# Scores and values of an attention on array tiles of 64 rows by 32 columns in place of 64 by 64

## The chip, the core and the metric

The kernel runs on one core of a Trainium2 chip. The metric is device time in microseconds (us) of one launch; the kernel before took 578.21 us, the median of 3 runs (577.76 to 578.54). TensorE (PE in the profile, its weight loads PEld) multiplies matrices and writes to the accumulators in PSUM, VectorE is DVE, ScalarE ACT, GpSimd POOL, and SyncE (SP) starts the DMAs.

## The reference, cut to what matters

Attention with a causal window of 128 positions and a linear bias, then a gated MLP over each batch. Batch 8, 8 heads, 576 positions, head dimension 64, all float32:

```python
scores = scale * np.matmul(q, k.transpose(0, 1, 3, 2))
rel = pos[:, None] - pos[None, :]
mask = (rel >= 0) & (rel < 128)
scores = np.where(mask, scores + bias[None], -1000000000.0)
attn = np.exp(scores - max); attn = attn / (sum + 1e-09)
x = (attn @ v), heads side by side                    # (8, 576, 512)
h = gelu(x @ w_in); u, v = halves of h
v_s = einsum('ts,bsd->btd', w_sg, layernorm(v) * g_ln) + b_sg
out = x + (u * v_s) @ w_out
```

## The kernel before, in words

The attention is done in 32 pairs of heads, numbered n: pair n is two heads of batch n // 4, one head on partitions 0 to 63 of the tile `qk` and the other on 64 to 127 (`heads`, L245). Queries are taken in nine blocks of R = 64. A query of a block can see the keys of its own block and of the two blocks before it, at most 192 keys. P is 128, T is 4.

`score_list` (L264) makes the products of a pair. Each is a `nc.tensor.matmul` of 64 rows (the head dimension) by 64 columns (the queries, as weights) by up to 192 streamed columns (the keys). So a product takes a quarter of the 128 by 128 array: the row half is the head's (`js`), the column half is given by where the result goes (`to`), and four products that differ in these use the four quarters. The list for `t2 = 0` has ten products: two of 128 columns, six of 192, two of 64 (the first block, which sees only itself); the list for `t2 = 2` has eight of 192. The results stand in two PSUM banks per list, the key window of the first block of queries (`i = 0`) in columns 0 to 191 and that of the second in 192 to 383.

`minima` (L297) has DVE merge the oldest and the newest 64 keys into one block of 64 (one of them is masked for each query), add the bias and take the minimum; then ACT takes exponentials, POOL or ACT scales them, PE transposes them (L347, L360), and DVE writes them, masked, to `px` (L356). `values` (L376) multiplies them by v: 18 products `part` and two products `first` per pair, each of 64 rows (64 keys), 64 columns (the head's 64 columns of v, as weights) and 64 to 192 streamed columns (queries), again on quarters: the row half by the key block's parity, the column half by the head j.

Weights and streamed data of scores and values are float32, and the trace has two weight loads and two matmuls (two passes) for each such product.

The other products are those of the MLP (L607 to L609, L796, L798, L905, L940, L941, L1059), on the whole array, 288 or 512 streamed columns.

The order of the work is a written list of steps, `ORDER` (L1150), in which a step is a letter and a pair: `*18` is both score lists of pair 18, `V16` the values of pair 16, `A`, `B`, `C`, `G` the four `minima`. Every engine takes its instructions in that order. For pairs 13 and 15 to 29 (`BEHIND`) the values of pair n come after the scores of pair n + 2 and one of their results is put in a free corner of that pair's score bank; for 15 to 29 no other product of PE stands between the two.

Of the kernel before, what the change touches and what calls it, by code (L numbers as in the profile page):

```python
# [21 lines left out]
def attention_gmlp(  # L22
# [17 lines left out]
    nc = tc.nc  # L40
    B, H, D, _, S = qkT.shape
    P = 128
# [4 lines left out]
    T = S // P  # L47
    R = S - T * P
    S2 = S // 2
    NPAIR = H // 2  # L50
    W = P
    EPS = 1e-6
# [20 lines left out]


    XW = 2 * S + R

    def hi_of(x):
        return x[:, 0:S]

    def lo_of(x):  # L80
        return x[:, S + R:XW]

# [10 lines left out]
    def halves(name, n, dt=F32):  # L93
        return const.tile([P, n], dt, name=name)
# [12 lines left out]
    alone, merged, plain = [rel[low, i * R:(i + 1) * R] for i in (0, 1, 2)]  # L107
# [9 lines left out]
    sel = halves("sel", 4 * R, U8)  # L117
# [4 lines left out]
    sel_first, sel = [sel[:, i * 2 * R:(i + 1) * 2 * R].rearrange("p (t c) -> p t c", t=2) for i in range(2)]  # L122

    biases = []
    for hp in range(NPAIR):
        x = halves(f"bias{hp}", 7 * R)
        nc.vector.tensor_scalar(x, rel, -slopes[2 * hp] * math.sqrt(D), None, ALU.mult)
        x = x.rearrange("p (b c) -> p b c", c=R)
# [17 lines left out]
    for i in range(2):  # L146
        x = const.tile([P, 2 * R], F32, name=f"e0_{i}")
# [5 lines left out]
    for i in range(3):  # L153
        x = const.tile([P, 2, NS], F32, name=f"stats{i}")
# [71 lines left out]
    def burst(insts):  # L226

        last = None
        for one in insts:
            if last is None:  # L230
                last = one()
            else:
                with tc.issue_after(last.ins):
                    last = one()

    class Pair:
# [26 lines left out]

        def score_list(self, t2, pool):  # L264
            qk, heads = self.qk, self.heads
            W = 3 * R
            if t2 == 0:
                self.pr = [att.tile([P, T, P], F32, name="e", bufs=4) for _ in range(2)]
                self.e0 = e0s[self.n % 2]
            if (self.n, t2) in IN_M:  # L270
                m = ps_m.tile([P, 2, 512], F32, name="ps_m")
                banks = self.banks[t2] = [m[:, i, :] for i in range(2)]
            else:
                banks = self.banks[t2] = [pool.tile([P, 512], F32, name=pool.name) for _ in range(2)]

            def score(half, j, c, q0, k0, k1):
                js, to = heads[j], heads[half ^ j]
                return lambda: nc.tensor.matmul(banks[half][to, c:c + k1 - k0], qk[js, 0, q0:q0 + R], qk[js, 1, k0:k1], start=True, stop=True)  # L278

            insts = []  # L280
            for i in range(2):
                for half in range(2):
                    for j in range(2):
                        q0 = (2 * t2 + 1 + i + 2 * half) * R
                        if q0 < P:
                            insts.append(score(half, j, i * W + R, q0, 0, P))
                        else:
                            insts.append(score(half, j, i * W, q0, q0 - P, q0 + R))
            if t2 == 0:
                insts += [score(0, j, 2 * W, 0, 0, R) for j in range(2)]  # L290
            return insts

        def shift(self, dst, src, bs, acc):
# [3 lines left out]
        def minima(self, t2, j):  # L297
            bank, pr, nm = self.banks[t2][j], self.pr, self.nm
            bias = biases[self.hp][j]
            sv = bank.rearrange("p (b c) -> p b c", c=R)  # L300
            alone = t2 + j == 0
            nc.vector.copy_predicated(sv[:, 0:6:5, :], sel_first if alone else sel, sv[:, 2:4, :])
            for i in range(2):
                bs = bias[:, 2:4, :] if i else bias[:, 0:3:2, :] if alone else bias[:, 1:3, :]
                self.shift(pr[j][:, t2 + i, :].rearrange("p (b c) -> p b c", b=2), sv[:, 4 * i:4 * i + 2, :], bs, nm[:, j * T + t2 + i:j * T + t2 + i + 1])
            if alone:
                self.shift(self.e0[:, R:P], sv[:, 6, :], bias[:, 0, :], nm[:, 2 * T:2 * T + 1])

        def exp(self, x, i):
            n = x.shape[0]  # L310
# [57 lines left out]
        def values(self):  # L368
            vt, px, heads = self.vt, self.px, self.heads
            if self.n in V_IN_S:  # L370
                x1 = [ps_s.tile([P, 512], F32, name="ps_s") for _ in range(2)]
            else:
                m = ps_m.tile([P, 2, 512], F32, name="ps_m")
                x1 = [m[:, i, :] for i in range(2)]
            self.x1 = x1
            behind = self.n in BEHIND  # L376
            x0 = self.x0 = pairs[BEHIND[self.n]].banks[2][1][:, 6 * R:7 * R] if behind else self.ct0[:, P:P + R]

            def part(k, j):
                i = 1 - k % 2  # L380
                rows, slot = slice(i * R, (i + 1) * R), (k + 1) // 2
                lo, hi = max(k - 1, 0), min(k + 2, 2 * T)
                c0 = (2 * P * (slot - 1) + P + i * R) if k else 0
                return lambda: nc.tensor.matmul(x1[i][heads[j], lo * R:hi * R], vt[rows, slot, heads[j]], px[rows, j * 2 * T * P + c0:j * 2 * T * P + c0 + (hi - lo) * R], start=k < 2, stop=k > 2 * T - 2, skip_group_check=True)  # L384

            def first(j):
                js, ks = heads[j], heads[1 - j if behind else 1]
                return lambda: nc.tensor.matmul(x0[js], vt[ks, 0, js], self.p0[ks, j * R:(j + 1) * R], start=True, stop=True)

            burst([part(k, j) for k in range(2 * T) for j in (1, 0)] + [x for j in (1, 0) for x in (part(2 * T, j), first(j))])  # L390

        def gather(self):
            nc.scalar.copy(self.xf[:, R:S], self.x1[0])
# [4 lines left out]
        def high(self):  # L398
            xs = self.xs = mlp.tile([P, XW], F32R, name="xs", bufs=NC)
            xss[self.b][self.hp] = xs  # L400
            nc.scalar.copy(hi_of(xs), self.xf)  # L401
# [4 lines left out]
        def low_tail(self):  # L406
# [7 lines left out]
            "R": inverse, "r": scale_first, "s": lambda p: p.scale(0), "S": lambda p: p.scale(1),  # L414
            "t": lambda p: p.transpose(0), "X": lambda p: p.masked(0), "z": transpose_first, "P": copy_first,
            "T": lambda p: p.transpose(1), "Y": lambda p: p.masked(1), "p": gather_first, "V": values, "x": gather, "2": gather_even, "h": high, "l": low, "k": low_tail,
        }

# [11 lines left out]
    class Planner:  # L430
# [7 lines left out]
        def add(self, name, engine, length, at, run, after=(), port=False, take=(), table=None, lag=0.22):  # L438
            assert name not in self.steps, name
            self.steps[name] = (engine, length, at, run, [x for x in after if x], port or engine == "POOL", list(take), table, lag)  # L440
# [688 lines left out]
    def idle_products(n, pool):  # L1129

        def run():
            if pool == "ps_m":
                m = ps_m.tile([P, 2, 512], F32, name="ps_m")
                banks = [m[:, i, :] for i in range(2)]
            else:
                banks = [{"ps_s": ps_s, "ps_a": ps_a}[pool].tile([P, 512], F32, name=pool)]
            for i in range(n):
                at = i // len(banks) % 2 * (512 - S2)
                nc.tensor.matmul(banks[i % len(banks)][:, at:at + S2], spare[:, 0:P], spare, start=True, stop=True)
        return run  # L1140

    for i, (n, pool) in enumerate(IDLE):
        add(f"W{i}", "PE", 0.13 * n, 0.0, idle_products(n, pool), [], take=[(pool, [f"W{i}"])])
    add_weights()
# [126 lines left out]
```

## Time and profile before

| | us |
|---|---|
| median of 3 runs | 578.21 |
| profiled execution: span from its first to its last instruction | 577.4 |
| PE busy in it | 560.8 (97%) |
| DVE busy | 473.8 (82%) |
| ACT busy | 378.6 (66%) |
| POOL busy | 308.0 (53%) |

The span is what the rows of the trace add up to; the time of a run has some 0.8 us around it. A busy PE can be one whose matmuls overlap, since a matmul's row lasts from its start to its modelled end, and up to four of them are in flight on quarters of the array; what a stretch of products costs is read from where the next one starts.

### The profile page before, as it was taken

To read this page: it belongs to the slowest core of one execution; us is meant where nothing else is said; L and a number is where in the kernel's file an instruction comes from. 1 tells how busy PE (TensorE), PEld (TensorE's weight loads), DVE (VectorE), ACT (ScalarE), POOL (GpSimd) and SP (SyncE) were. 2 spreads that over 40 slices of the span, in tenths; PEclk is the share of its full clock that TensorE was granted. 3 is DMA by queue.
4 is the path that set the end of the run, shared out by engine and by line. 5 is a ranking of instruction groups with operands and counts; after the bars stand their busy time and mean duration, and the time that the engine had idled before them with its cause. 6 is when DMAs were issued, how large, how long until landed. Compare 5 with 4: busy or idle time off the path is not lost.

```text
span 577.4 us, 14654 instructions
## 1 busy us (share of the span) xinstructions
PE 560.8 (97%) x5495; PEld 512.7 (89%) x5495; DVE 473.8 (82%) x1324; ACT 378.6 (66%) x1063; POOL 308.0 (53%) x365
## 2 busy tenths in 40 slices
PE   5889999999999999999999999999999999999997
PEld 4667899998899799997999998998989999998997
DVE  7989998799989868899788987878897988666646
ACT  7988997466853867467776576746695667833422
POOL 3676646530436543575447753496347653576325
PEclk9989999999999999999999999999999999999999
DMA  8675213216403413454260465135332606012502
GB/s 297 190 235 199 72 45 121 69 46 243 167 37 125 156 37 99 146 192 129 60 212 10 140 204 173 43 103 168 130 120 65 214 2 197 2 35 96 171 1 82
DMA packets 43561, 69.78 MB, mean 121 GB/s; under 512 B 3554, under 2 KB 31202, under 8 KB 43492
## 3 DMA queue, kind: packets, MB, share of 16 engines
q1 hardware_dynamic: 43492, 68.86, 36.7%
q8 instruction: 43, 0.70, 0.5%
q14 instruction: 26, 0.21, 0.1%
HBM read 56.27 MB, written 12.58 MB: 119 GB/s over the span
## 4 chain that ended last, share of the span: by engine, by line
PE 90%; DVE 5%; DMA 2%; ACT 1%; issue 1%; POOL 0%; SPq 0%; DVEq 0%; ACTq 0%
PE ps_m L607 13%; PE ps_m L1059 13%; PE ps_m L609 12%; PE ps_m L608 12%; PE ps_m L905 12%; PE ps_a L347 5%; PE ps_s L384 4%; PE ps_s L278 4%; PE ps_a L278 4%; PE ps_m L384 3%; DMA qk<-qkT 2%; PE ps_m L941 2%; PE ps_m L940 1%; DVE px L356 1%; DVE e L295 1%; PE ps_m L796 1%
## 5 line engine op out<-in xcount | busy, mean ns | idle before, releaser
L334 POOL TENSOR_TENSOR e<-e,rr 128x256 f32<-128x256 f32 (+2 forms) x116 | 80.7, 718 | 97.0 <-DVE rr L323 84.9
L311 ACT ACTIVATE e<-e,stats 128x128 f32<-128x128 f32 (+1 forms) x288 | 110.6, 386 | 17.7 <-DVE stats L295 17.1
L224 POOL TENSOR_TENSOR region<-u,region 128x288 fp32r<-128x288 f32 (+1 forms) x78 | 77.7, 1016 | 44.7 <-ACT region L1006 16.2
L356 DVE TENSOR_TENSOR px<-ps_a,m_both 128x1024 f32<-128x1024 f32 x64 | 77.4, 1216 | 5.9 <-PE ps_a L347 5.4
L607 PE MATMUL ps_m<-ws,region 128*128 128x288 f32 x256 | 78.2, 306 | 0.0
L609 PE MATMUL ps_m<-ws,region 128*128 128x288 f32 x256 | 75.7, 296 | 0.0
L608 PE MATMUL ps_m<-ws,region 128*128 128x288 f32 x256 | 75.6, 295 | 0.0
L730 POOL TENSOR_TENSOR rs<-rs,mhalf 128x1 f32<-128x1 f32 (+1 forms) x40 | 30.2, 756 | 57.4 <-DVE rs L727 57.2
L218 POOL TENSOR_TENSOR xs<-xf,xs 128x288 fp32r<-128x288 f32 (+1 forms) x48 | 49.9, 1060 | 13.8 <-ACT xs L401 13.8
L311 ACT ACTIVATION_READ_ACCUMULATOR e<-e,stats 128x1 f32 x288 | 54.4, 189 | 0.0
L1006 ACT ACTIVATE region<-u 128x576 fp32r<-128x576 f32 x35 | 23.7, 684 | 43.4 <-PE ps_m L608 17.4
L607 PEld LDWEIGHTS ps_m<-ws,region 128*128 128x128 f32 x256 | 48.3, 189 | 1.5 <-issue 0.8
L608 PEld LDWEIGHTS ps_m<-ws,region 128*128 128x128 f32 x256 | 48.2, 188 | 0.1
L609 PEld LDWEIGHTS ps_m<-ws,region 128*128 128x128 f32 x256 | 48.1, 188 | 0.1
L607 PE MATMUL ps_m<-wi,xs 128*128 128x512 f32 x112 | 46.9, 418 | 0.1
L1066 DVE TENSOR_TENSOR xf<-ps_m,xf 128x576 f32<-128x576 f32 x48 | 35.7, 750 | 10.9 <-PE ps_m L1059 10.1
L609 PE MATMUL ps_m<-wi,xs 128*128 128x512 f32 x112 | 44.3, 395 | 0.0
L608 PE MATMUL ps_m<-wi,xs 128*128 128x512 f32 x112 | 44.2, 395 | 0.0
L946 DVE TENSOR_TENSOR u<-ps_m,u 128x576 f32<-128x576 f32 x32 | 24.0, 752 | 18.7 <-PE ps_m L941 11.5
L347 PE MATMUL ps_a<-ident,e 128*128 128x128 f32 x256 | 38.0, 275 | 1.0 <-DVE px L356 1.0
L295 DVE CUSTOM_DVE_ANT_0 e<-ps_s,bias 128x128 f32<-128x128 f32 (+1 forms) x140 | 34.9, 287 | 2.5
L278 PE MATMUL ps_s<-qk 64*64 64x192 f32 (+2 forms) x576 | 31.5, 333 | 5.3 <-DMA qk<-qkT 4.9
(217 smaller groups left out, 1600.9 us busy)
## 6 DMA issues: line engine op xcount, KB each, us to landing
qk<-qkT SPq DMA_DIRECT2D x32, 576.0 KB, 4.7
sum<-store SPq DMA_DIRECT2D x36, 512.0 KB, 4.8
outT<-xf SPq DMA_DIRECT2D x31, 288.0 KB, 3.0
vt<-v_in SPq DMA_DIRECT2D x32, 256.0 KB, 4.1
wst<-w_in SPq DMA_DIRECT2D x8, 512.0 KB, 4.8
store<-sum SPq DMA_DIRECT2D x6, 512.0 KB, 2.7
vt<-v_in SPq DMA_DIRECT2D x64, 32.0 KB, 4.2
wst<-w_out SPq DMA_DIRECT2D x4, 512.0 KB, 3.6
```

Source lines behind the costliest of these rows:

```text
L218: (engine or nc.gpsimd).tensor_tensor(out[:, cs], a[:, cs], b[:, cs], op)
L224: nc.gpsimd.tensor_tensor(out[:, fs], a[:, fs], b[:, fs], ALU.subtract)
L278: return lambda: nc.tensor.matmul(banks[half][to, c:c + k1 - k0], qk[js, 0, q0:q0 + R], qk[js, 1, k0:k1], start=True, stop=True)
L311: nc.scalar.activation(x, x, AF.Exp, bias=self.nm[0:n, i:i + 1], scale=-1.0, accum_out=self.sm[0:n, i:i + 1])
L334: nc.gpsimd.tensor_tensor(x[:, z:z + step, :], y[:, z:z + step, :], self.rr[0:n, i + z:i + z + min(k, step)].rearrange("p (m o) -> p m o", ...
L347: burst([lambda t=t: nc.tensor.transpose(cv[:, t // 2, t % 2], self.pr[j][:, t, :].rearrange("p (h c) -> p h c", h=2), ident[:, j * R:j * ...
L356: nc.vector.tensor_tensor(xv, cv, mv, ALU.mult)
L607: nc.tensor.matmul(dst, ah, bh, start=(first and i == 0), stop=False)
L608: nc.tensor.matmul(dst, ah, bl, start=False, stop=False)
L609: nc.tensor.matmul(dst, al, bh, start=False, stop=(last and i == n - 1))
L905: nc.tensor.matmul(dst, left(n, g, c)[:, ms], right(n, h, c), start=first and c == 0 and k == 0, stop=c == 1 and k == 2, skip_group_check= ...
L1059: nc.tensor.matmul(dst, p, q, start=first and f == 0 and k == 0, stop=f == 1 and k == 2, skip_group_check=True)
```

## The change

The products of scores and values are cut into two each, by columns of the array. A score product now has 32 queries as weights in place of 64. Since a block of 32 queries sees at most 128 + 32 = 160 keys, it streams 160 columns in place of 192; in the first list the products of the first full block stream 96 and 128 columns in place of 128, and those of the very first block 64 as before. A value product now has 32 columns of v as weights in place of 64, and streams as many columns as before. The results land on 32 partitions each, at the same partitions as before; in the score banks the windows of the two query blocks now begin 160 columns apart (BAND), those of the second 32 queries of a block 32 columns further, and the first block's window moves to column 352 (LEAD). DVE's instructions keep their count and sizes and read at other columns.

```diff
+    BAND = 5 * R // 2
+    LEAD = 2 * BAND + R // 2
+
+    def window(bank, c0, c1):
+        x = bank[:, c0:c0 + R].rearrange("p (t c) -> p t c", t=1)
+        return bass.AP(tensor=x.tensor, offset=x.offset, ap=[x.ap[0], [c1 - c0, 2], x.ap[2]])
...
-            def score(half, j, c, q0, k0, k1):
-                js, to = heads[j], heads[half ^ j]
-                return lambda: nc.tensor.matmul(banks[half][to, c:c + k1 - k0], qk[js, 0, q0:q0 + R], qk[js, 1, k0:k1], start=True, stop=True)
+            half_block = R // 2
+
+            def score(half, j, c, q, k0, k1):
+                js, to = heads[j], heads[half ^ j].start + q % R
+                return lambda: nc.tensor.matmul(banks[half][to:to + half_block, c:c + k1 - k0], qk[js, 0, q:q + half_block], qk[js, 1, k0:k1], start=True, stop=True)
...
-                        q0 = (2 * t2 + 1 + i + 2 * half) * R
-                        if q0 < P:
-                            insts.append(score(half, j, i * W + R, q0, 0, P))
-                        else:
-                            insts.append(score(half, j, i * W, q0, q0 - P, q0 + R))
+                        for z in (0, half_block):
+                            q0 = (2 * t2 + 1 + i + 2 * half) * R
+                            lo = max(q0 + z - P, 0)
+                            insts.append(score(half, j, i * BAND + lo - q0 + P, q0 + z, lo, q0 + z + half_block))
             if t2 == 0:
-                insts += [score(0, j, 2 * W, 0, 0, R) for j in range(2)]
+                insts += [score(0, j, LEAD, z, 0, R) for j in range(2) for z in (0, half_block)]
...
-            nc.vector.copy_predicated(sv[:, 0:6:5, :], sel_first if alone else sel, sv[:, 2:4, :])
+            nc.vector.copy_predicated(window(bank, 0, BAND + P), sel_first if alone else sel, window(bank, P, BAND))
...
-            def part(k, j):
+            def part(k, j, z):
                 i = 1 - k % 2
-                rows, slot = slice(i * R, (i + 1) * R), (k + 1) // 2
+                rows, slot, ds = slice(i * R, (i + 1) * R), (k + 1) // 2, slice(j * D + z, j * D + z + D // 2)
...
-            burst([part(k, j) for k in range(2 * T) for j in (1, 0)] + [x for j in (1, 0) for x in (part(2 * T, j), first(j))])
+            split = [(j, z) for j in (1, 0) for z in (0, D // 2)]
+            burst([part(k, j, z) for k in range(2 * T) for j, z in split] + [x for j, z in split for x in (part(2 * T, j, z), first(j, z))])
```

On PE, at the place where both score lists of pair 18 (tile `qk`, written to the PSUM tiles `ps_a` and `ps_s`) and behind them the values of pair 16 (tiles `px` and `vt`, to `ps_m`) stand between two products of the MLP, the program before had these rows. Each gives the line, the tiles, the size of the result (weights' columns by streamed columns) and how many follow one another:

```order
L798 MATMUL ps_m<-wi,xs 64x512 x4
L278 MATMUL ps_a<-qk 64x128 x2
L278 MATMUL ps_a<-qk 64x192 x6
L278 MATMUL ps_a<-qk 64x64 x2
L278 MATMUL ps_s<-qk 64x192 x8
L384 MATMUL ps_m<-px,vt 64x128 x2
L384 MATMUL ps_m<-px,vt 64x192 x12
L384 MATMUL ps_m<-px,vt 64x128 x2
L384 MATMUL ps_m<-px,vt 64x64
L388 MATMUL ps_s<-p_1_120,vt 64x64
L384 MATMUL ps_m<-px,vt 64x64
L388 MATMUL ps_s<-p_1_120,vt 64x64
```

In the changed program the same place on PE, with the lines moved down by 5 to 7, reads:

```order
L805 MATMUL ps_m<-wi,xs 64x512 x4
L285 MATMUL ps_a<-qk 32x96
L285 MATMUL ps_a<-qk 32x128
L285 MATMUL ps_a<-qk 32x96
L285 MATMUL ps_a<-qk 32x128
L285 MATMUL ps_a<-qk 32x160 x12
L285 MATMUL ps_a<-qk 32x64 x4
L285 MATMUL ps_s<-qk 32x160 x16
L390 MATMUL ps_m<-px,vt 32x128 x4
L390 MATMUL ps_m<-px,vt 32x192 x24
L390 MATMUL ps_m<-px,vt 32x128 x4
L390 MATMUL ps_m<-px,vt 32x64
```

Behind these come seven more rows of 32 by 64 products, `part` and `first` by turns. The 18 score products are 36 and the 20 value products 40; none stands at another place among the other products, and the other engines have the same instructions in the same order as before.

## Rows read from the trace of the kernel before

**Rows 1.** The page: busy time by engine, and the chain that ended last.

```profile
PE 560.8 (97%) x5495; PEld 512.7 (89%) x5495; DVE 473.8 (82%) x1324; ACT 378.6 (66%) x1063; POOL 308.0 (53%) x365
...
PE 90%; DVE 5%; DMA 2%; ACT 1%; issue 1%; POOL 0%; SPq 0%; DVEq 0%; ACTq 0%
```

**Rows 2.** Stretch, length; PE, PEld, DVE, ACT, POOL busy (count); clock; DMA share; GB/s.

```profile
0.00:60.00 60.00, 48.76 (x497) 38.71 (x498) 51.44 (x184) 52.55 (x165) 36.21 (x42) 0.97 0.68 222
60.00:120.00 60.00, 60.00 (x674) 55.20 (x673) 52.37 (x165) 46.25 (x149) 34.61 (x33) 1.00 0.24 75
120.00:240.00 120.00, 119.10 (x1122) 108.15 (x1121) 104.26 (x271) 75.44 (x199) 49.59 (x50) 1.00 0.37 124
240.00:360.00 120.00, 119.19 (x1244) 109.57 (x1243) 102.18 (x310) 82.24 (x246) 67.30 (x84) 1.00 0.42 137
360.00:500.00 140.00, 140.00 (x1434) 131.17 (x1433) 116.44 (x326) 93.94 (x264) 78.84 (x110) 1.00 0.34 108
```

**Rows 3.** Whom PE waited for between 60 and 500 us: total, times, longest.

```profile
PE ps_m L905 <- PE ps_m L905: 0.9, 1, 0.9
PE ps_a L278 <- DMA qk<-qkT: 0.8, 1, 0.8
```

**Rows 4.** The chain, 83.2 to 85.3 us: a pair's scores between products of the MLP.

```profile
83.36 0.14 PE ps_m L941
83.49 0.80 PE ps_a L278 x18
84.30 0.66 PE ps_s L278 x16
84.95 0.33 PE ps_m L607
85.28 0.13 PE ps_m L608
```

**Rows 5.** The chain, 254.9 to 258.3 us: scores with values right behind them.

```profile
254.99 0.81 PE ps_a L278 x18
255.80 0.66 PE ps_s L278 x16
256.45 1.19 PE ps_m L384 x28
257.64 0.06 PE ps_s L388
...
257.76 0.12 PE ps_s L388 x2
257.88 0.38 PE ps_a L347 x2
```

**Rows 6.** The chain, 98.8 to 101.1 us: a pair's values by themselves.

```profile
98.87 0.11 PE ps_a L360
98.98 1.51 PE ps_s L384 x36
100.49 0.12 PE ps_a L388 x4
100.60 0.48 PE ps_a L347 x3
```

**Rows 7.** Score products' matmuls and weight loads in flight, after PE had waited for a DMA.

```profile
264.71:264.74 0.03, 0.00 (x0) 0.03 (x1) 1.00 0.00 0
264.74:264.77 0.03, 0.03 (x4) 0.03 (x5) 1.00 1.98 819
```

**Rows 8.** Weight loads by line and shape (64 and 128 columns): count, busy, mean ns.

```profile
L607 PEld LDWEIGHTS ps_m<-ws,region 128*128 128x128 f32 x256 | 48.3, 189 | 1.5 <-issue 0.8 <-DVE u L946 0.3
L384 PEld LDWEIGHTS ps_m<-px,vt 64*64 64x64 f32 x612 | 24.6, 133 | 0.9 <-issue 0.2
```

**Rows 9.** The chain's longer pieces of scores before 60 us.

```profile
4.86 1.62 PE ps_s L278 x18
21.07 0.87 PE ps_s L278 x18
36.99 0.81 PE ps_s L278 x16
```

## What I expected before the run

> **What bounds the kernel now.** I read the page's busy times and its chain of waits first [rows 1]: PE is busy for 97% of the span, and 90% of the chain that ended last is PE's own work. Then the stretches [rows 2]: from 60 to 500 us PE is busy for 438.3 of 440 us, while DVE, the next engine, reaches 87% at most (104.26 of 120 us), ACT and POOL less, and the clock granted to PE is 1.00. In the same 440 us PE waited for others for 1.7 us [rows 3]. So in the middle of the kernel a nanosecond taken from PE's instructions is nearly a nanosecond of the time, and one added is a nanosecond lost. Before 60 us PE has 11 us of gaps, and what is won there is mostly waited away again.
>
> **What a product costs now.** A matmul's row overlaps with three others, so its length says little; the chain gives what a list takes until the next work begins. The second score list, eight products of 192 columns on the four quarters of the array, two passes each (16 records), takes 0.66 us [rows 4]. Each quarter runs two products, so four passes: 0.66 / 4 = 0.164 us a pass, 0.855 ns a column. That is two cycles a column at 2.4 GHz, the clock granted there. The four quarters therefore run side by side all the time and there is no slack in the list that a better order could take. The first list bears this out: its longest quarters have the same four passes of 192 (or as many columns in 128 and 192) and the quarters of the first block two of 64 more, and it takes 0.80 us, 0.14 more, where 128 columns by 0.855 are 0.11 and the rest is the start. So a pass is paid by its columns, and a shorter one is cheaper.
>
> **Scores, where the MLP follows.** The change halves the columns of weights and so doubles the tiles to eight; if all eight run side by side, a tile's time is again its own sum of streamed columns. First list: the longest quarter had 2 x (128 + 192 + 64) = 768 columns; the longest tile now has 2 x (128 + 160 + 64) = 704 (its twin 640). Second list: 4 x 192 = 768 become 4 x 160 = 640. Together 192 columns less, by 0.855 ns 0.16 us per pair. In the chain after 60 us the scores of 11 pairs stand like this [rows 4], and one more pair in two separate lists: 12 x 0.16 = 1.9 us.
>
> **Scores with values right behind.** For 15 pairs the values follow without a gap [rows 5], and the tile that counts is the one with the largest sum over both. Before, it is the one on rows 64 to 127 and output columns 0 to 63: 8 x 192 = 1536 for scores and 2 x (128 + 3 x 192 + 64 + 64) = 1664 for values, 3200 columns by 0.855 = 2.74 us of the 2.89 us from 254.99 to 257.88. After, its two halves have 1280 + 1664 = 2944; the tiles that are longest in the scores (704 + 640) have 1536 of values, 2880. The saving is 256 columns, 0.22 us: 15 x 0.22 = 3.3 us.
>
> **Values.** They stream what they streamed: 1664 columns on the longest tile, 1.42 us of the 1.62 us from 98.98 to 100.60 [rows 6]. I cost the split at nothing in either place; its use is that scores and values stay in one form of tiles. It costs if the eight tiles don't run side by side, which is priced below.
>
> **Twice the instructions.** 38 products become 76 per pair, 152 matmuls and as many weight loads. After PE had waited for a DMA, four matmuls came into flight within 30 ns, with five loads [rows 7], so under 10 ns for a matmul and its load. Four more tiles to start cost up to 30 ns at the start of a stretch of such products; there are some 40 such stretches after 60 us, up to 1.2 us. Against it stands the first weight load, which nothing hides: loads of 128 and 64 columns last 189 and 133 ns [rows 8], 56 ns for 64 columns, so one of 32 should be some 28 ns shorter, up to 1.1 us back. I take zero, and keep +1.2 and -1.1.
>
> **What else moves.** Nothing changes its place on any engine's list, the DMAs and SP's queue included. DVE's merge reads two windows of 64 columns as before, only 160 columns apart; its cost I take as unchanged. PE's products are all drained once per stretch before and after, as the forms still alternate with the whole array equally often. What waits for scores (DVE's merge) or values (ACT's copy) gets them earlier.
>
> **Before 60 us** three pieces of the chain are scores [rows 9]: the first list at 4.86 us, twice as long as its like later (1.62 against 0.81 us), may give 0.11 us, the two others 0.05 and 0.11: 0.3 us.
>
> **The sum.** 1.9 + 3.3 + 0.3 = 5.5 us of PE. I let 90% of it come through, as short waits that PE's pace hides now will show, of which there are two already [rows 3]: 4.9 us. The profiled execution's span is 577.4 us; it becomes 572.5. The median of the runs, 578.21, stands 0.8 us above the span; with that the forecast is 573.3 us. Its own range: all of 5.5 and the 1.1 of shorter loads, 571.6; 70% and the 1.2 of starts, 575.6.
>
> **Rivals.** First, and on the other side: PE doesn't get the doubled number of products going fast enough. Place: all 32 pairs, in the scores and values. Point from which it decides: 152 matmuls in the 2.89 us of [rows 5] are one each 19 ns; every nanosecond above that costs 152 x 32 = 4.9 us. For it: the densest steady rate that the trace has is that of [rows 5], 76 matmuls in 2.89 us, 38 ns; were that a limit of issue, it would be 19 x 4.9 = 93 us, 671. Against: those 76 are explained to 5% by columns alone (2.74 us), so the array and not the issue set that rate, and the four within 30 ns [rows 7] are far below 19 ns. I stand with [rows 7], the nearer row, since it has the same kind of products on different tiles; chance 0.12. The Trainium skill, TensorE: Matmul & The Clock Gate, section "Wait — 56ns, not 53.3ns?", gives the rule that speaks against this change: the starts of two matmuls are never less than about 25 ns apart, however few columns they stream. By that rule, as an estimate, 6 x 4.9 us are lost, about 608 us; the trace disagrees for starts on different tiles, with four in 30 ns, and can't say whether eight hold that pace for long.
>
> Second: no more than two column tiles of one row half run at a time; no row shows a third. Then two twins take turns, their columns add up, and the longest pair of tiles has 704 + 640 + 640 + 640 = 2624 columns of scores and 3328 of values against 1536 and 1664: 2752 more, 2.35 us, by 32 pairs 75 us, 653. Against: the two column halves of a row half have their own streams now and don't slow each other at all, and nothing in the trace sets two as the end of it. Chance 0.08. The Trainium skill, TensorEngine Tiling (Array Packing), section "Available Configurations", lists 64 by 32 as eight independent tiles; no run here shows it yet.
>
> Third: the scores get shorter and PE then waits for DVE, whose 87% from 120 to 240 us is the next limit. All of the gain gone is 578.2. Against: DVE has 16 us free in those 120, and PE would run some 1.6 us ahead in them. Chance 0.08.
>
> **How the numbers follow.** Forecast 0.72, issue rate 0.12, shared streams 0.08, PE waits for DVE 0.08. The measurement can tell some 0.2% (1.2 us) from no change. Faster: 0.72 and a quarter of the third rival, 0.74; same: most of the rest of it, 0.05; slower: the first two and a little of the third, 0.21. The range takes the forecast's lower end, 571.6, and reaches up over the third rival to 578.6; what lies above it has about 0.2.
>
> **What would show it.** In the profile after: the second score list in the chain at about 0.55 us in place of 0.66, the first at about 0.75; scores with values at 2.67 us in place of 2.89; values alone at 1.6 as now. If the issue rate rules, the lists grow instead, in proportion to their matmuls, values alone to over 1.6 us; if streams are shared, values alone take about 3 us. If DVE takes over, PE's lists are short as forecast and gaps with DVE as releaser stand on PE between 120 and 360 us. The forecast is wrong if the score lists are not shorter, or if they are and PE's waits after 60 us exceed some 3 us.

## The result, and the profile after

The changed kernel took 584.76 us, the median of 4 runs (582.28 to 585.2); the kernel before took 578.0 us beside it (577.76 to 578.54). The ratio is 1.0105, with a 95% interval of 1.0091 to 1.0119: slower by 1.1%, where 573.3 us was forecast. The profiled execution has a span of 583.4 us, 6.0 more than before; the medians differ by 6.8 us, and what follows explains the 6.0 between these two executions.

The page of the changed kernel answers to [rows 1]. Its third row here is the DMA queue that brings instructions: transfers, MB, share of the 16 engines' span.

```profile
PE 559.5 (96%) x7927; PEld 511.4 (88%) x7927; DVE 474.3 (81%) x1324; ACT 378.0 (65%) x1063; POOL 308.1 (53%) x365
...
q8 instruction: 62, 1.02, 0.8%
...
PE 88%; DVE 5%; ACT 2%; DMA 2%; issue 2%; POOL 1%; SPq 0%; DVEq 0%; POOLq 0%
```

The kernel before had in that queue, on its own page:

```profile
q8 instruction: 43, 0.70, 0.5%
```

PE is busy for 1.3 us less than before, so the products as such did get cheaper; the time went into idling, and "issue" in the chain grew from 1% to 2%. The queue tells more: PE and PEld together have 10,990 rows before and 15,854 after. The change needs 4,864 rows and 19 transfers more, which is 256 rows to a transfer: PE's instructions come in blocks of 256, 16 KB each.

The lists first. Chain of the changed kernel, 83.9 to 86 us (start, length, what), for [rows 4]:

```profile
84.08 0.68 PE ps_a L285 x28
84.76 0.71 PE ps_s L285 x31
85.46 0.33 PE ps_m L614
```

Chain, 286 to 289.5 us, scores with values, for [rows 5]:

```profile
286.21 0.68 PE ps_a L285 x28
286.89 0.63 PE ps_s L285 x29
...
287.60 1.14 PE ps_m L390 x48
...
288.92 0.11 PE ps_s L394 x4
289.03 0.43 PE ps_m L614
```

Chain, 99.2 to 101.4 us, values alone, for [rows 6]:

```profile
99.42 1.46 PE ps_s L390 x61
...
100.91 0.11 PE ps_a L394 x7
101.02 0.48 PE ps_a L353 x3
```

Scores alone went from 1.46 us to 1.39 (forecast 1.30), scores with values from 2.89 to 2.82 (forecast 2.67), values alone from 1.62 us to between 1.59 and 1.60 in most places (forecast 1.6). The eight tiles do run side by side, else values alone had doubled. But less than half of the saving is there: 11 pairs of score lists at 0.073 us, 0.18 us for the pair whose two lists stand apart, 15 stretches of scores with values at 0.067 where nothing stops, and 0.33 us in 11 of the 13 stretches of values come to 2.3 us behind 60 us, and not 5.2.

Then the idling. Whom PE waited for in the changed kernel from 60 to 506 us (total, times, longest), for [rows 3]:

```profile
PE ps_m L390 <- issue: 2.2, 1, 2.2
PE ps_s L394 <- issue: 1.5, 2, 0.9
PE ps_a L285 <- DMA qk<-qkT: 1.2, 1, 1.2
PE ps_m L912 <- PE ps_m L912: 1.0, 1, 1.0
```

The last two rows are the two of [rows 3], the one for `qk` 0.4 us longer. The first two are new, 3.7 us in which PE's next value products wait for nothing that the profile shows. The chain of the changed kernel from 483 to 490 us has the longest:

```profile
483.24 0.68 PE ps_a L285 x28
483.92 0.63 PE ps_s L285 x29
...
485.83 0.03 PE ps_s L394
485.86 0.00 PE ps_m L390
485.86 2.19 issue
488.05 0.32 PE ps_m L390 x2
```

PE stops in the middle of a list of like products, near the end of 152 that follow one another. Taken by where a stretch begins and the next other product starts, four late stretches of scores with values take 3.06 (at 431.8 us), 3.59 (445.1), 3.97 (462.9) and 5.45 us (483.2) in place of 2.82; one at 254.8 us takes 3.33. The transfers of the changed kernel while PE stands still at 485.9 us show what is late. In the stretch 482.50 to 485.37 (DMA share by fortieths, then the queues):

```profile
DMA  9597969798998969896989899598999999999996
...
q1 hardware_dynamic: 864, 1.09, 102.9%
```

and in the stretch 485.37 to 486.48:

```profile
DMA  9222222110000000000000000000000000000010
...
q8 instruction: 1, 0.02, 6.1%
q1 hardware_dynamic: 44, 0.02, 5.9%
```

While 1.09 MB of `v` and `sum` fill the 16 engines no instructions come at all. The block is fetched from 485.38 on, when the data is through, and PE goes on some 1.6 us after it has landed at 486.47.

What standing still costs further is in the windows of the changed kernel (start:end, length, busy time and count of PE, PEld, DVE, ACT, POOL, granted clock, DMA share, GB/s):

```profile
486.47:488.05 1.58, 0.00 (x0) 0.00 (x0) 0.10 (x2) 0.05 (x1) 1.17 (x3) 0.96 0.00 0
488.05:491.30 3.25, 3.25 (x19) 3.08 (x19) 2.10 (x3) 0.59 (x1) 0.00 (x0) 0.50 0.34 98
491.30:494.00 2.70, 2.70 (x17) 2.40 (x17) 0.87 (x2) 1.78 (x6) 0.00 (x0) 0.99 0.80 240
```

After 2.2 us without a product the clock is at 0.50, the level of 1.2 GHz, for 3.3 us of full work.

So the 6.0 us are made up like this. At 62 us the changed kernel is 0.72 us behind, by a stop of the same kind in the chain at 33 us (the kernel before loses time at this place too: its clock stands at 0.50 from 31.29 to 34.71 us of its profile, which the changed kernel's does not):

```profile
31.48 1.55 PE ps_s L390 x59
...
33.09 0.06 PE ps_a L394 x3
33.15 2.03 issue
35.18 0.21 PE ps_a L394
```

Over the next 354 us the shorter lists win some 1.2 us, and the stop in the stretch at 254.8 us and the longer wait for `qk` behind it take 0.8 of it back: at 416 us it is 0.32 behind. The four late stretches then are 0.17 + 0.71 + 1.08 + 2.57 = 4.5 us longer than 2.885 us each, and about 1.2 us go to the half clock: 0.3 + 4.5 + 1.2 = 6.0.

### The profile page after: what moved, and what is told of

It is laid out like the page before. It is cut to its first block, busy times and chain, and to the rows that moved or that the text cites. A ratio compares the mean times of both kernels' runs of the same rounds, so it can differ in the third digit from the quotient of the medians.

```text
span 583.4 us, 19518 instructions
## 1 busy us (share of the span) xinstructions
PE 559.5 (96%) x7927; PEld 511.4 (88%) x7927; DVE 474.3 (81%) x1324; ACT 378.0 (65%) x1063; POOL 308.1 (53%) x365
## 4 chain that ended last, share of the span: by engine, by line
PE 88%; DVE 5%; ACT 2%; DMA 2%; issue 2%; POOL 1%; SPq 0%; DVEq 0%; POOLq 0%
PE ps_m L1066 13%; PE ps_m L614 12%; PE ps_m L912 12%; PE ps_m L616 12%; PE ps_m L615 12%; PE ps_a L353 5%; PE ps_m L390 4%; PE ps_s L390 4%; PE ps_s L285 3%; PE ps_a L285 3%; PE ps_m L948 1%; PE ps_m L947 1%; ACT e L317 1%; PE ps_m L803 1%; DMA wst<-w_in 1%
## 5 line engine op out<-in xcount | busy, mean ns | idle before, releaser
L285 PE MATMUL ps_s<-qk 64*32 64x160 f32 (+2 forms) x1152 | 32.3, 306 | 5.0 <-DMA qk<-qkT 4.4
```

The source lines that it names most:

```text
L285: return lambda: nc.tensor.matmul(banks[half][to:to + half_block, c:c + k1 - k0], qk[js, 0, q:q + half_block], qk[js, 1, k0:k1], start=Tru ...
```

## The experiments

The theory (A): the products are not slower, but PE runs through its instructions faster than its next block of 256 comes, where many small products stand together and where data is moved at the same time. The rivals: a dense run of small products on eight tiles is itself too much for PE; one half of the change, scores or values, is at fault; the data transfers hold up PE or its partners in either kernel.

**Scores alone narrow.** The changed kernel with the values of before:

```diff
...
-            burst([part(k, j, z) for k in range(2 * T) for j, z in split] + [x for j, z in split for x in (part(2 * T, j, z), first(j, z))])
+            burst([part(k, j) for k in range(2 * T) for j in (1, 0)] + [x for j in (1, 0) for x in (part(2 * T, j), first(j))])
```

> Scores on tiles of 64 by 32 as in the change, values on 64 by 64 as before. Theory A (PE runs out of instructions: they come in blocks of 256 by DMA, a stretch of scores with values behind now takes 304 of them in 2.8 us, and a block that has to wait behind data leaves PE with nothing to issue): such a stretch has 224 instructions here, so few or no gaps put down to issue inside the stretches, scores by themselves 1.39 us as after, and with a drain between the two forms some 2.9 us for scores with values: 576 to 580 us. Theory B (the gaps belong to the form of 64 by 32 itself, eight tiles with their queues): gaps of 0.5 us and more as after in the same late stretches, 581 us or more.

578.78 us, ratio 1.0011 (1.0002 to 1.0021). No new wait of PE. Chain of this kernel, 284.8 to 287.9 us:

```profile
284.88 0.68 PE ps_a L285 x28
285.56 0.71 PE ps_s L285 x31
286.27 1.40 PE ps_m L390 x34
...
287.72 0.12 PE ps_s L394 x3
287.84 0.43 PE ps_m L613
```

Scores with values take 2.96 us, where scores alone take 1.39 and values alone 1.62: where 64 by 32 tiles are followed by 64 by 64 ones, the two lists overlap by 0.05 us. In the kernel before they overlap by 0.20 us (1.46 + 1.62 against 2.89), in the changed one by 0.16 (1.39 + 1.59 against 2.82). So this half of the change alone has no stops, and gives its 0.07 back in the chained places.

**Values alone narrow.** The kernel before with the changed values:

```diff
...
-            burst([part(k, j) for k in range(2 * T) for j in (1, 0)] + [x for j in (1, 0) for x in (part(2 * T, j), first(j))])
+            burst([part(k, j, z) for k in range(2 * T) for j, z in split] + [x for j, z in split for x in (part(2 * T, j, z), first(j, z))])
```

> Values on tiles of 64 by 32 as in the change, scores on 64 by 64 as before; no product streams less. Theory A: 232 instructions in a stretch of scores with values, few gaps; values by themselves 1.59 us against 1.62; 577 to 581 us. Theory B: gaps of 0.5 us and more in the late stretches where values run, 581 us or more.

580.94 us, ratio 1.0045 (1.0028 to 1.0061). No stop either; values alone 1.59 us, scores with values 3.04, with an overlap of 0.01 us. Its loss of 3.0 us is mostly this missing overlap, 15 x 0.15 us. Neither half alone makes the 6 us, so neither is at fault by itself: the stops come with both together.

**Twice the products on the old tiles.** The kernel before, streams of 128 and 192 columns cut in two:

```diff
...
-                            insts.append(score(half, j, i * W, q0, q0 - P, q0 + R))
+                        insts += [score(half, j, c, q0, lo, mid), score(half, j, c + mid - lo, q0, mid, hi)]
...
-            burst([part(k, j) for k in range(2 * T) for j in (1, 0)] + [x for j in (1, 0) for x in (part(2 * T, j), first(j))])
+            burst([part(k, j, y) for k in range(2 * T) for j in (1, 0) for y in (0, 1)] + [x for j in (1, 0) for x in (part(2 * T, j, 0), first(j, 0))])
```

> Tiles of 64 by 64 as before, but each score product and each value product of 128 or 192 streamed columns cut into two of half the columns: 70 products per pair in place of 38, and the same columns. Theory A: 280 instructions in a stretch of scores with values, so gaps put down to issue as after, of 0.3 to 3 us in some late stretches, and slower than before: 580 to 586 us. Theory B: no tile of 32 columns, so no gaps; 577 to 579 us.

584.52 us, ratio 1.0112 (1.0097 to 1.0127). The time is what A expected, the reason in the main is not: after 60 us no product stops for instructions. Instead every stretch is longer, scores alone 1.65 us and scores with values 3.10. The cut costs 0.19 us in the scores of a pair and 0.22 us where values follow, and with it 280 rows of PE and PEld are used in 3.10 us, where the changed kernel uses 304 in 2.82. So more instructions alone don't make a stop in every dense stretch. That the slower pace is what avoids them fits theory A, but the blocks end at other places too, so for the late stretches this run doesn't show it. Before 60 us, however, this kernel has one such stop, in a score list of 64 by 64 tiles. Its chain from 51.8 us:

```profile
51.76 0.39 PE ps_s L278 x13
52.15 0.59 issue
52.74 0.59 PE ps_s L278 x17
```

The block that PE needed there was fetched from 50.49 to 51.45 us. So it takes no tile of 32 columns to make a stop, which is against the rival that puts it on eight tiles.

**Scores and values apart.** The changed kernel, with a step of the MLP put between the scores and the values of the 15 chained pairs:

```diff
...
-    for n, run in plan.run(ORDER.split()):
+    for n, run in plan.run(apart(ORDER.split())):
```

> The changed kernel, but for the 15 pairs whose values stand right behind scores an MLP step of PE (1.6 to 3 us or more) is put between the two. Theory A: no stretch has more than 160 instructions before the array's long products follow, so blocks come in time: no gap over 0.3 us put down to issue after 60 us. 15 stretches become two, 1.39 + 1.59 in place of 2.82 us, 15 x 0.16 = 2.4 us more; the gaps and the half clock they brought (6 to 7 us) go: 579 to 582 us. Theory B: gaps remain as after and the 2.4 us come on top: 586 us or more.

607.95 us, ratio 1.052 (1.0504 to 1.0535), far outside. The stops of the late stretches are gone, but the new order costs more than it frees; this kernel's PE waits from 60 to 500 us begin with

```profile
PE ps_m L614 <- ACT vg L793: 7.7, 5, 2.7
PE ps_m L1066 <- DVE xf L403: 1.7, 3, 0.8
```

since steps that other engines need come later. The test says nothing on A's size.

**Moving the block ends.** 56 more instructions at the start of PE's list, products on data at hand, so that every later block ends 56 instructions earlier in the program:

```diff
+    def first_products(n):
+        def run():
+            bank = ps_m.tile([P, 2, 512], F32, name="ps_m")[:, 0, :]
+            for i in range(n):
+                nc.tensor.matmul(bank[:, 0:P], spare[:, 0:P], spare[:, 0:P], start=True, stop=True)
+        return run
+    add("W99", "PE", 0.1, 0.0, first_products(28), [], take=[("ps_m", ["W99"])])
...
```

> The changed kernel with 28 small products (128 columns, 56 instructions of PE) put ahead of everything, while PE waits for its first DMA; nothing else differs, but every later instruction stands 56 places further against the blocks of 256 in which they are fetched. In the changed kernel PE stopped at the last instruction of a block (place 448 behind the block's start) at 447, 465 and 485 us. Theory A (a stretch of 304 instructions runs dry where the fetch of the next block happens to begin at its start): those three gaps and the half clock behind the last one go, at most one of some 0.5 us appears near 300 us: 576.5 to 579 us. Theory B (the gaps come from data DMAs or from the eight tiles at those moments, wherever the blocks end): gaps at the same three places, 584 us or more.

585.58 us, ratio 1.0125 (1.0111 to 1.0139), against 576.5 to 579 expected: the time missed. The late stops are gone, as expected; in this kernel's chain the stretch that corresponds to the one at 483 us has none:

```profile
487.38 0.68 PE ps_a L285 x28
488.06 0.63 PE ps_s L285 x29
...
490.09 0.11 PE ps_s L394 x4
490.20 0.59 PE ps_a L353 x4
```

It has another instead, at 270 us, where none was before and none was expected:

```profile
269.07 1.14 PE ps_m L390 x48
270.23 2.59 issue
272.82 0.31 PE ps_m L390
```

and from 264 to 270 us its DMA engines moved 1.60 MB of data at 90% and no instructions at all. The start, too, came out 2.1 us later than in the changed kernel. These 2.1 us, the new stop and the half clock behind it about make up for the stops that went. The same products at the same place stop or don't stop with the place of the block's end: that is against a list that is too dense in itself.

**Narrow only where nothing chains.** Scores on 64 by 32 tiles for pairs 0 to 16, the rest as before:

```diff
+    NARROW = range(17)
...
+        def score_list(self, t2, pool):
+            return (self.score_list_narrow if self.n in NARROW else self.score_list_wide)(t2, pool)
```

> Scores on tiles of 64 by 32 for pairs 0 to 16 alone, whose scores stand by themselves; scores of pairs 17 to 31 and all values on 64 by 64 as before. From the parts measured so far: 11 stretches after 60 us of 1.39 in place of 1.46 us (-0.8), the start about 0.7 us earlier as with scores alone, scores with values 2.885 us as before, no gaps: 576.0 to 577.2 us. If the shorter scores are worth nothing once other engines follow: 577.5 to 578.5.

577.67 us, ratio 0.999 (0.9981 to 0.9999), span 576.3: 0.1% below the kernel before, less than expected. It has no stop. It is 1.2 us ahead at 61 us and 1.1 us at the end. The lead at 61 us can't be put down to its lists: the control with the old lists at the end of this section is 1.0 us ahead there too. Of what the 11 score lists between save, 0.8 us at 0.07 each, 0.2 were still there at 253 us, and none of it at 415. Of what shorter lists save in the middle, little arrives.

**The order of the narrow products.** The same with score products sorted so that each goes to the tile that comes free first, and the same sorting in the changed kernel:

```diff
...
-                insts += [score(0, j, LEAD, z, 0, R) for j in range(2) for z in (0, half_block)]
+                at = [(0, 0, z0), (0, 0, z1), (0, 1, z0), (0, 1, z1), (1, 0, z0), (1, 0, z1), (1, 1, z0), (1, 1, z1)]
+            else:
+                at = [(0, 0, z0), (0, 1, z0), (0, 1, z1), (0, 0, z1), (1, 0, z0), (1, 1, z0), (1, 1, z1), (1, 0, z1)]
...
```

> As the kernel with pairs 0 to 16 alone on 64 by 32, and within each score list the products are ordered by when their tile comes free, which the forecast took for granted. Theory: PE starts products in their order, and one whose tile is busy holds up those behind it for idle tiles, which is why scores by themselves took 1.39 us and not the 1.30 forecast. Then they take 1.30 to 1.33 us here and the whole 0.6 to 1.0 us less than with the old order, 575.2 to 576.5 us. Rival: the eight tiles share something (streams or weight loads), 1.39 us as before the new order and the same time as without it.

577.45 us, ratio 0.9994 (0.9985 to 1.0002), scores alone 1.38 us, not the 1.30 to 1.33 expected: the order is not what keeps them from 1.30.

> The changed kernel with score products ordered by when their tile comes free, nothing else. Same number of PE instructions in every stretch, so Theory A expects the gaps at the same places (447, 465, 485 us) and as long or longer; scores by themselves 1.30 to 1.33 us, scores with values 2.67 to 2.75 in place of 2.82: 581 to 583.5 us. Rival (shared streams): 1.39 and 2.82 us, 584 to 585.5.

582.8 us, ratio 1.007 (1.0051 to 1.0088). Scores with values come to 2.75 us, and three of the stretches with a stop still have it: 3.59 at 253.6, 3.32 at 461.3 and 5.09 at 481.0 us. The stop of the stretch at 443.9 us falls just behind it, on the MLP's products, and those at 33 and 432 us are gone.

**The data taken out of the way.** The changed kernel and the kernel before, both with 36 reloads of 512 KB cut to 4 KB (so that later batches are computed with old sums; only the time counts):

```diff
-        return lambda: nc.sync.dma_start(sums[i].bitcast(F32), store[number][:, i])
+        return lambda: nc.sync.dma_start(sums[i][0:1].bitcast(F32), store[number][0:1, i])
```

> The changed kernel, in which 36 reloads of 512 KB into the tiles `sum` are cut to one partition each (4 KB): the outputs from the second batch on are computed with old sums, and their time alone counts. Theory A (PE stops where the fetch of its next block of instructions isn't back, and this fetch starts late while the DMA engines are full of data): the stretch of scores and values near 483 us, in the middle of two of these reloads, shrinks from 5.454 to 3.5 to 3.8 us, the half clock behind it goes, the stretch near 254.8 us goes from 3.33 to about 2.82; the two near 445 and 463 us, where no such reload runs, keep their 3.6 and 4.0 us. Time 581 to 582.5, against 584.8 for the changed kernel. Rival B (the stop has nothing to do with the DMAs, PE simply can't take products at this pace in that place): the stretch near 483 us stays at 5.3 to 5.6 us and the time within 584 to 585.5.

> The kernel before with the same 36 reloads cut to 4 KB each (outputs from the second batch on use old sums). The control to the run beside it. Theory A: PE is not held by these loads there, and scores with values stay at 2.88 us: 577.3 to 578.5, no change beyond 0.2%. Rival C (the reloads themselves hold up PE or its partners in both kernels): it gets faster by as much as the changed kernel does, 2 to 4 us, 574 to 576.

The changed kernel without the reloads: 580.7 us, ratio 1.0039 (1.0026 to 1.0052), 0.3 us below what was expected; its runs lie between 579.1 and 582.1 us. The kernel before without them: 577.9 us, ratio 1.0 (0.999 to 1.0009). So the reloads cost the kernel before nothing and the changed one some 4 us, which a limit of PE's own can't give, nor transfers that hold up either kernel. The chain of the changed kernel without reloads:

```profile
482.86 0.68 PE ps_a L285 x28
483.54 0.63 PE ps_s L285 x29
...
485.48 0.28 issue
485.75 0.25 PE ps_m L390 x2
```

and its transfers from 482.97 to 484.21 us:

```profile
q8 instruction: 1, 0.02, 6.1%
q1 hardware_dynamic: 45, 0.02, 5.0%
```

The block that came from 485.38 on with the reloads now comes from 482.98 on; the stretch takes 3.31 us in place of 5.45, and no half clock follows. Of 3.4 us won behind 483 us, 2.1 are the stretch and 1.2 what lies behind it. The stretches at 445 and 463 us, where no reload runs, take 3.37 and 3.71 (3.59 and 3.97 with them), as expected nearly the same: there the fetch comes too late without any load beside it. The stretch near 255 us went to 2.82 as expected, but not for that reason: the fetch before it still started 5.2 us late, behind other data, and PE came 0.8 us later, after a stop of 1.5 us at 34 us.

## Why the prediction was wrong

**Twice the instructions** is the step that failed. It said "I take zero, and keep +1.2 and -1.1", and priced only how fast products start and load once PE has them. It did not ask how the instructions get to PE. Behind 60 us alone the term came to some 6.5 us: five stretches take 5.3 us more than 2.82 us each, and the half clock costs 1.2. The starts were priced rightly in kind: eight tiles keep going at 2.82 us for 152 matmuls, 18.5 ns each, and a load of 32 columns lasts 106 to 109 ns in the trace after, 24 to 27 ns less than one of 64, where 28 were estimated from [rows 8]. The Trainium skill, TensorE: Matmul & The Clock Gate, section "Wait — 56ns, not 53.3ns?", has about 25 ns as the least distance of two starts; on different tiles this run goes below that for a whole stretch.

What was missing is the supply. With PE's rows numbered from 0 in order of time, the 205 of its sequencer among them, the six stops of the changed kernel, at 33, 255, 432, 445, 463 and 483 us, stand right behind row 256k + 448 (k = 2, 28, 49, 51, 53, 55), and so do the stop at 270 us of the kernel with shifted blocks (k = 30) and the one at 52 us of the kernel with cut streams (k = 4). The instruction transfer numbered k, from 0, was never seen to start before row 256k + 152 of the changed kernel. PE goes through these 296 rows in 2.6 to 3.0 us at 445, 463 and 483 us, and the transfer needs its own start (about 1.0 us at 445 and 463, 2.7 at 483 behind data, 0.7 there without the reloads), 1.0 to 1.4 us of its own, and 1.3 to 1.6 us until PE goes on: 3.4 to 3.7 us, and 5.4 at 483. In the kernel before PE takes 11.3 us at least for the same 296 rows, with scores alone narrow 5.5 and with values alone narrow 7.0 (in the streams that were cut, 4.4 us behind 60 us). In none of the twelve traces does the first row behind 256k + 448 run earlier than 1.2 us after its block has landed; in the kernel before it runs 6.4 us after it or later, and no stop was seen.

**Scores, where the MLP follows**, and **Scores with values right behind**: right in sign and mis-sized, 0.07 us each in place of 0.16 and 0.22. The columns went as counted, but what a stretch takes beyond its longest tile's columns grew: in scores with values 2.885 - 2.74 = 0.15 us before, and 2.818 - 2944 x 0.855 ns = 0.30 us after; in scores alone 0.15 and 0.24. The prediction had 0.03 us for that ("up to 30 ns at the start"). In the one pair whose two lists stand apart, at 62.7 and 66.0 us of the changed kernel, the lists go from 0.81 us each to 0.74 and 0.70: 0.18 us, all that the columns give. So the 0.1 to 0.15 us come in where one list joins the next; why stays open. The order of the products is 0.01 to 0.06 of it (the two sorted kernels).

**Values** at nothing: 0.03 us better than that in most places.

**Before 60 us**: the changed kernel is 0.7 us behind, by its stop at 33 us, where 0.3 ahead was forecast. What the lists save there is not shown: the kernel with only scores narrow is 0.7 us ahead at 61 us and the one with them in pairs 0 to 16 1.2, but the kernel before with short reloads, which has the old lists and no reload before 100 us, is 1.0 ahead as well. All three lack the half clock that the profile of the kernel before has from 31.29 to 34.71 us.

**The sum**: "90% of it come through" was too much. Without stops, from 299.7 to 416.3 us, seven stretches saved 0.47 us and PE got 0.33 ahead; in the kernel with narrow scores for pairs 0 to 16 a quarter of the middle's 0.8 us came through, and none to the end. So even without the stops the 2.3 us behind 60 us would have given at most some 1.6.

**The rivals**: the first had the right side, and its place (the dense stretches), but not its mechanism: it expected each product to start late, in every list, and the lists are shorter. The second (shared streams) is refuted by values alone at 1.59 us. The third didn't show: PE waits no more for DVE than before. "PE's waits after 60 us exceed some 3 us" was named as a sign against the forecast, and that is what came.

## What to carry to other kernels

Where a change multiplies an engine's instructions, ask not only what one costs but how fast they are used up against how fast they come: divide the engine's rows by the transfers of the instruction queue on the page, and see how long the densest stretch takes for one block and what data moves beside it. A list of like products that stops in its middle with "issue" as its releaser, at the same row of every block and just after a transfer of the instruction queue has landed late, is that case; data moved beside it at 483 us and none at 445. Narrow tiles did no harm here where other products give the fetch time, but two widths in one stretch cost 0.07 to 0.15 us each time.

## What was not expected of the hardware

- Blocks of 256 instructions (16 KB): 60 of the changed kernel's 62 transfers took 0.9 to 1.4 us, the longest 2.8 us. They began up to 8.4 us after row 256k + 152 (from 24 us on, with the DMA engines busy at 85% with data; from 248 us on it was 6.3 us).
- 64 by 32 tiles followed by 64 by 64 ones, or the other way round, hardly overlap: 1.39 + 1.62 us against 2.96, and 1.46 + 1.59 us against 3.04, an overlap of 0.05 and 0.01 us, where tiles of one form overlap by 0.16 to 0.20 us.
- Products cut in two on 64 by 64 tiles made a stop of 0.6 us as well, at 52 us.
- A stop of 2.2 us was followed by 3.3 us at 0.50 of the clock, a stop of 2.6 us by 3.2 us (in the kernel with shifted blocks), and the changed kernel's shorter stops and its 2.0 us at 33 us by none; in the sorted kernel one of 2.0 us, at 483.7 us, was followed by 3.4 us at 0.50 that began about 1 us after it had ended.
